# The last 64 output columns first, and two accumulators in one tile

## The chip, the cores and the metric

The kernel runs on one core of one Trainium2 chip. The metric is the device time of one execution in microseconds (us). Its engines are PE (matmuls), DVE (vector), ACT (scalar), POOL (general purpose) and SP, which here issues the DMA transfers. Matmul results land in PSUM, which has eight banks of 512 float32 per partition.

## What is computed

`x` has 8 batches of 3584 rows of 192 columns. A 7-tap convolution per head, whose weights are a softmax over the taps, gives 28672 rows, and these go through a soft mixture of 8 experts with 4 slots each (32 slots), F = 1024:

```
out    = einsum('bshk,bskhg->bshg', softmax(weight_gen), windows of x)   # -> x: 28672 x 192
logits = x @ phi                                    # 28672 x 32
d      = softmax of logits over the rows            # dispatch
slot_input = d.T @ x                                # 32 x 192
slot_out[e] = relu(slot_input[e] @ w1[e]) @ w2[e]   # per expert, 4 x 192
c      = softmax of logits over the slots           # combine
result = c @ slot_out                               # 28672 x 192
```

## The kernel before

The rows are cut into 17 units of eight pairs of groups and a short last one. In the main loop (about 25 to 217 us) each unit passes through these steps, each with its engine:

- `conv` (L263, PE) by banded weights that DVE turns (L236) from what POOL multiplied; then transposes (L283, PE).
- `logits` (L339, PE) into the PSUM tile `ls`, one bank.
- `top` (L346, DVE), `newmax` (L365, PE) and `newmax_out` (L370, DVE): the running maximum.
- `dexp` (L378, ACT): exponentials of `ls` into `dd`; `dturn` (L398, DVE): `dd` transposed into `dt`.
- `save` (L352, DVE): `ls` transposed into `LT` in the on-chip memory (SBUF), for the combine softmax later. In program order it follows `dturn` on the DVE.
- `dispatch` (L417, PE): 16 matmuls of `dt` with the unit's rows into `acb`, a PSUM tile of its own, one bank; `rescale` (L425, DVE) adds it to `accS`.

Three further tiles of two banks each, `ring0` to `ring2`, take the convolutions and transposes in turn. That fills the eight banks.

Then comes the slot stage (217 to 231.6 us), written out by hand: slot sums (L861 to L871), `hidden` (L905) in two halves u = 0, 1 with a relu and a transpose each (`turn_hidden`, L917 on PE and L918 into `hT`), `den` and `rden` (L939 to L953), the divisor, and `outputs` (L926): per expert and quarter a matmul of `hT` with `w2`, for the first DA = 128 of the D = 192 columns, into `so4`. The copy `sos` (L964), the sum over the four quarters (L968) and the scaling by `rden` (L969) give `so`.

The output stage makes 25 parts, in the order of `out_order`. A part of kind 0 is 128 columns of one half batch, one of kind 1 the last 64 columns of two half batches; both fill 128 partitions. A part is `rows` (L994, PE, into two PSUM tiles `two` of two banks, four of them in turn), `evict` (L1000, copies by ACT and DVE into free SBUF) and `store` (L1005, issued by SP; the first three parts in two stores each). The last 64 columns (`others`, `other_sums`) are made behind the fifth and sixth part. Between them stand the last combine softmaxes: maximum L92 (DVE), difference L94 (POOL), exponential L97 (ACT), sum L100 (DVE), L102 (ACT), reciprocal L104 (DVE), product L106 (POOL), and `turn` (L475, DVE), which transposes a half batch into `cT` for `rows`.

The order on the engines in the loop and in the output stage comes from a planner: every step is declared by `op(engine, cost, reads, writes, ...)`, `times` lays them on the engines by these costs, and the steps are written in the order of their planned times. Each engine runs its instructions in that order. Waits between engines are set by the framework, from which tiles an instruction reads and writes.

Of the kernel before, what the change touches and what calls it, by code (L numbers as in the profile page):

```python
# [8 lines left out]
F32 = mybir.dt.float32  # L9
# [27 lines left out]
FILL = 2  # L37
WGAP = 0.9
TR = 3 * 32 + T
RESTAT = 4  # L40
BEHIND = 6
ROUNDS = {"TE": 8, "SP": 12}
VSUM = ()
# [13 lines left out]
def conv_soft_moe(ctx, tc, xh, wh, phi, w1a, w1b, w2a, w2b, out):  # L57
# [16 lines left out]
    big = keep.tile([128, NXS * XB], F32, name="big")  # L74
    FC = F // 128
    WE = FC * D
    W2B = E * FC * DA

    DG = NS + SE
    si = keep.tile([128, E * NS + E // 2 * DG], F32, name="si")  # L80
# [43 lines left out]
    tms = [fix.tile([128, UP, 2 * (D + 1)], F32, name=f"tm{i}") for i in range(NTM)]  # L124
    tms.append(wide.rearrange("p b j -> p (b j)")[:, 0 : TAIL * 2 * (D + 1)].rearrange("p (n c) -> p n c", c=2 * (D + 1)))
    dd = fix.tile([128, 2 * UP, 32], F32, name="dd")
    ls = ps_fix.tile([128, 2 * UP, 32], F32, name="ls")


    acb = ps_fix.tile([128, 512], F32, name="acb")  # L130
    qnegP = acb[:, 264:268]

    banks = [ps_fix.tile([128, 2, 512], F32, name=f"ring{i}") for i in range(NRING)]
# [342 lines left out]
                    LT[:, g0 : g0 + n].rearrange("p g j -> p (g j)"))  # L476

    def w2_at(e, f, b):
        o = W2B * b + (e * FC + f) * (D - DA if b else DA)
        return big[:, o : o + (D - DA if b else DA)]  # L480

    def loadw1(j):
        e, f = j // 4, slice(F // 4 * (j % 4), F // 4 * (j % 4 + 1))
        to, w, e = (w1a_sb, w1a, e) if e < E else (w1b_sb, w1b, e - E)
        SY.dma_start(to[:, e, f], w[:, e, f])

    W2S = [(0, i * 4 * DA, 4 * DA) for i in range(2 * E)]
# [363 lines left out]
    half = F // 8  # L851

    spare = [banks[(used[0] + 1 + i // 2) % NRING][:, i % 2] for i in range(4)]
    homes = {"b1": acb, "b3": spare[0], "b4": spare[1], "b2": spare[2], "b0": spare[3]}

    def bank(tag, n, name):
# [84 lines left out]
    rden = pb.tile([128, 1], F32, name="rden")  # L941
    hidden(1, E // 2, E + E // 2)
# [19 lines left out]
    soft(pc, h + 1, 6)
    soft(pc, h + 2, 3)
    V.tensor_copy(sos[:, 0:DA], so4)  # L964
    soft(pc, h + 2, 4)
    soft(pc, h + 2, 5)
    sor = bank("b2", DA, "sor")
    P.matmul(sor, sel4.rearrange("p q s -> p (q s)"), sos[:, 0:DA], start=True, stop=True)  # L968
    V.tensor_scalar_mul(so, sor, rden[:, 0:1])  # L969
    soft(pc, h + 2, 6)  # L970
    turn(1, 0)
    bctx.close()


    ps_o = ctx.enter_context(tc.tile_pool(name="ps_o", bufs=4, space=PSUM))
# [6 lines left out]
    assert RESTAT + 2 < len(spots)  # L982
    spots += [big[:, i * OW : (i + 1) * OW] for i in range(E * WE // OW)]
    parts = list(out_order())
    pos, left = {}, [0]

    def rows(kind, b, g, n, j):
        pos[j] = [ps_o.tile([128, 2, 512], F32, tag="two", name=f"two{j}_{i}") for i in range(2)]
        for half in range(1 + kind):
            g0 = NG * (b + half) + g  # L990
            of = (so, sob)[kind]
            m = of.shape[1]
            for q in range(4):
                P.matmul(pos[j][q // 2][m * half : m * half + m, q % 2, 0 : n * T],  # L994
                         of[32 * q : 32 * q + 32],
                         cT[32 * q : 32 * q + 32, g0 : g0 + n, 0:T], start=True, stop=True)
# [12 lines left out]
    extra = []

    def others(u):
        if u == 0:
            extra.append(ps_o.tile([128, 2, D - DA], F32, tag="two", name="extra"))
        outputs(extra[0][:, 0], 1, (u,), 0, E)

    def other_sums():
        P.matmul(extra[0][:, 1], sel4.rearrange("p q s -> p (q s)"), sos[:, DA:D], start=True, stop=True)

    ops.clear()
    writer.clear()  # L1020
    readers.clear()
    op(VE, 0.74, [], [("cT", 3)], turn, 1, 1)
    for x in range(EARLY + 3, len(HALVES)):
        for step, (e, c) in enumerate(((VE, 0.72), (PO, 1.13), (AC, 0.66), (VE, 0.72),
                                       (AC, 0.3), (VE, 0.25), (PO, 1.13))):
            op(e, c, [], [("soft", x), ("rm", x % 2)], soft, pc, x, step)
        op(VE, 0.74, [("soft", x)], [("cT", x)], turn, x // 2, x % 2)
    twos = [0]

    def turn_two():  # L1030
        twos[0] += 1
        return ("two", twos[0] % 4)

    for j, (kind, b, g, n) in enumerate(parts):
        two, to = [turn_two(), turn_two()], ("spot", j % len(spots))
        op(TE, (1.1 + 0.8 * kind) * (n + 6) / 24, [("cT", 2 * (b + half) + (g >= STEPS[1][0])) for half in range(1 + kind)]
           + ["sob"] * kind, two, rows, kind, b, g, n, j)
        cuts = ((0, 2, AC), (2, 4, VE)) if j < 3 else ((0, 2, AC), (3, 4, VE), (2, 3, AC))
        free = ["w2"] * (j >= RESTAT + 2)
        for lo, hi, e in cuts:  # L1040
            if e == AC:
                op(AC, 0.14 + 0.4 * (hi - lo) * n / 18, [two[lo // 2], *free], [(to, lo)], evict, j, n, lo, hi, A.copy)
            else:
                op(VE, 0.12 + 0.52 * (hi - lo) * n / 18, [two[1], *free], [(to, lo), ("ev", j)], evict, j, n, lo, hi, V.tensor_copy)
        if 4 <= j + 2 < EARLY + 3:
            op(VE, 0.74, [("ev", j)], [("cT", j + 2)], turn, (j + 2) // 2, j % 2)
# [3 lines left out]
        if j == RESTAT:  # L1050
            rest = turn_two()
            op(TE, 1.05, [], [rest], others, 0)
        elif j == RESTAT + 1:
            op(TE, 1.05, [], [rest, "w2"], others, 1)
            op(AC, 0.22, [rest], ["sos"], lambda: A.copy(sos[:, DA:D], extra[0][:, 0]))
            op(TE, 0.4, ["sos"], [rest], other_sums)
            op(VE, 0.22, [rest], ["sob"], lambda: V.tensor_scalar_mul(sob, extra[0][:, 1], rden[:, 0:1]))
# [95 lines left out]
```

## Time and profile before

| | |
|---|---|
| median of 3 runs | 295.62 us (295.34 to 295.69) |
| profiled execution, its own time | 294.6 us |
| its span, first to last instruction | 292.5 us |
| busy share of PE, DVE, ACT, POOL | 88%, 73%, 62%, 55% |
| written to HBM | 22.36 MB |
| mean granted clock of PE | 0.949 |

A granted clock of 1.00 is the full 2.4 GHz, 0.50 is 1.2 GHz. Rows of a timeline give start and length in us from the span's start; a bracket at the end is the idle time of the engine before the row, and what ended it. Where several instructions of one kind follow each other, one row holds them, with their count behind an x.

### The profile page before, as it was taken

How to read it: one execution, taken by the hardware profiler on the slowest of the kernel's cores; microseconds unless marked ns; L12 is line 12 of the kernel's file. 1: busy time of each engine (PE TensorE's matmuls, PEld its weight loads, DVE VectorE, ACT ScalarE, POOL GpSimd, SP SyncE). 2: the span in 40 equal slices, each digit the busy share in tenths (PEclk: the TensorE clock that was granted, in tenths of full speed). 3: DMA queues.
4: the chain of work that ended last, by engine and by line, in shares of the span. 5: the costliest groups of instructions: out<-in, count | busy, mean ns of one | idle time of the engine just before them, and what ended most of it. 6: DMA issues, size and time to landing. Idle time of an engine off the chain costs nothing.

```text
span 292.5 us, 16099 instructions
## 1 busy us (share of the span) xinstructions
PE 258.0 (88%) x6996; PEld 209.2 (72%) x6996; DVE 212.7 (73%) x385; ACT 180.9 (62%) x307; POOL 160.4 (55%) x253
## 2 busy tenths in 40 slices
PE   8789998999899999999999999999989798856520
PEld 4579898888799898988988898998869553311100
DVE  8776999876998887788858688773374888977310
ACT  8868657576577756656665666665322378968430
POOL 9974869468496775657374735720034415555100
PEclk9999999999999999999999999999999889975675
DMA  6986677677667766767777668666988099999994
GB/s 178 233 220 175 189 230 205 175 214 211 198 174 205 215 201 192 209 187 211 223 220 207 201 196 232 187 199 168 303 269 288 14 385 407 416 423 413 416 413 185
DMA packets 30406, 70.11 MB, mean 240 GB/s; under 512 B 5760, under 2 KB 17024, under 8 KB 30336
## 3 DMA queue, kind: packets, MB, share of 16 engines
q1 hardware_dynamic: 30336, 69.08, 74.3%
q8 instruction: 55, 0.90, 1.3%
q14 instruction: 15, 0.12, 0.1%
HBM read 46.70 MB, written 22.36 MB: 236 GB/s over the span
## 4 chain that ended last, share of the span: by engine, by line
PE 74%; issue 5%; ACT 4%; DMA 4%; POOL 4%; DVE 3%; POOLq 0%; ACTq 0%
PE ring L263 33%; PE ring L283 16%; PE ls L339 8%; PE acb L417 7%; PE two L994 6%; PE ring L905 2%; DMA taps<-wh 2%; DMA out<-w1b_sb 2%; ACT big L1000 1%; POOL big L433 1%; ACT w1a_sb L1000 1%; DMA out<-w1a_sb 1%; POOL LT L106 1%; DVE band L236 1%; ACT w1b_sb L1000 1%
## 5 line engine op out<-in xcount | busy, mean ns | idle before, releaser
L263 PE MATMUL ring<-big,band 128*26 128x96 f32 x4480 | 109.7, 248 | 3.9 <-DVE band L236 2.0
L263 PEld LDWEIGHTS ring<-big,band 128*26 128x26 f32 x4480 | 99.5, 130 | 13.3 <-issue 6.8
L271 ACT COPY tm<-ring 128x768 f32<-128x768 f32 x68 | 54.5, 801 | 57.9 <-PE ring L263 45.2
L236 DVE STREAM_TRANSPOSE band<-wide 128x832 f32<-128x832 f32 x70 | 70.6, 1025 | 4.6 <-POOL wide L227 3.3
L283 PE MATMUL ring<-ident,tm 122*128 122x122 f32 x408 | 50.4, 273 | 0.8 <-issue 0.8
L227 POOL TENSOR_TENSOR wide<-taps,sum 128x364 f32<-128x364 f32 x32 | 31.4, 982 | 25.9 <-DVE sum L218 10.2
L289 ACT COPY cm<-ring 128x624 f32<-128x624 f32 x68 | 44.1, 691 | 1.9 <-PE ring L283 1.9
L283 PEld LDWEIGHTS ring<-ident,tm 122*128 122x128 f32 x408 | 42.3, 141 | 3.7 <-issue 0.9
L196 POOL TENSOR_TENSOR taps<-taps,top 128x364 f32<-128x364 f32 x34 | 32.9, 974 | 4.4 <-DVE top L188 4.2
L994 PE MATMUL two<-cT,so 32*128 32x442 f32 (+2 forms) x136 | 23.0, 701 | 11.6 <-DVE cT L475 3.9
L212 POOL TENSOR_TENSOR si<-taps 128x208 f32<-128x208 f32 x34 | 21.8, 640 | 19.9 <-ACT taps L204 19.4
L188 DVE TENSOR_REDUCE top<-taps 128x52 f32<-128x364 f32 x34 | 27.9, 822 | 4.2 <-DMA taps<-wh 4.1
L94 POOL TENSOR_TENSOR LT<-LT,rm 128x576 f32<-128x576 f32 (+1 forms) x16 | 18.1, 1133 | 20.5 <-DVE rm L92 20.3
L339 PE MATMUL ls<-cm,phi_sb 128*32 128x208 f32 x544 | 27.2, 338 | 0.0
L417 PE MATMUL acb<-tm,dt 128*32 128x193 f32 x544 | 25.8, 328 | 0.0
L994 PEld LDWEIGHTS two<-cT,so 32*128 32x128 f32 x136 | 9.2, 224 | 23.1 <-ACT w1a_sb L1000 8.3
L106 POOL TENSOR_TENSOR LT<-LT,sm 128x576 f32<-128x576 f32 (+1 forms) x16 | 18.1, 1134 | 13.1 <-DVE sm L104 13.1
L204 ACT ACTIVATE taps<-taps 128x364 f32<-128x364 f32 (+1 forms) x36 | 18.0, 503 | 7.9 <-POOL taps L196 7.0
L218 DVE RECIPROCAL sum<-sum 128x52 f32<-128x52 f32 (+1 forms) x36 | 16.3, 454 | 8.9 <-POOL sum L214 8.6
L339 PEld LDWEIGHTS ls<-cm,phi_sb 128*32 128x32 f32 x544 | 17.5, 109 | 4.2
L1000 ACT COPY big<-two 128x884 f32<-128x884 f32 (+3 forms) x26 | 17.2, 738 | 4.4 <-issue 3.5
L346 DVE TENSOR_REDUCE mx<-ls 128x1 f32<-128x416 f32 x17 | 9.8, 577 | 13.7 <-PE ls L339 12.4
(135 smaller groups left out, 298.4 us busy)
## 6 DMA issues: line engine op xcount, KB each, us to landing
big<-xh SPq DMA_DIRECT2D x224, 120.0 KB, 3.6
taps<-wh SPq DMA_DIRECT2D x35, 182.0 KB, 3.7
out<-big SPq DMA_DIRECT2D x7, 884.0 KB, 9.1
out<-big SPq DMA_DIRECT2D x6, 936.0 KB, 9.4
w1a_sb<-w1a SPq DMA_DIRECT2D x32, 128.0 KB, 3.4
big<-w2a SPq DMA_DIRECT2D x16, 256.0 KB, 4.3
out<-w1a_sb SPq DMA_DIRECT2D x3, 936.0 KB, 10.7
w1b_sb<-w1b SPq DMA_DIRECT2D x16, 128.0 KB, 3.3
```

Source lines behind the costliest of these rows:

```text
L188: V.tensor_reduce(out=row(m), in_=run(c, 0, KT).rearrange("p k s -> p s k"), axis=AX.X, op=ALU.max)
L196: eng.tensor_tensor(out=t, in0=t, in1=rows7(tops.pop((c, 0))), op=ALU.subtract)
L227: eng.tensor_tensor(out=dst, in0=raw[c % NTAP][:, 0:KT], in1=m.unsqueeze(1).to_broadcast([128, KT, n, T]), op=ALU.mult)
L236: V.transpose(bands[c % NBAND][:, b].rearrange("p b j l -> p (b j l)"), wide[:, b].rearrange("p b j -> p (b j)"))
L263: P.matmul(cv[32 * blk : 32 * blk + T, p % 2, o : o + 4 * GW], bands[g // 8 % NBAND][:, g // 4 % CH, :, i], xbd[:, place(t), :, b * GW : ( ...
L271: copy(tms[tm_at(u)][:, pr + of.start : pr + of.stop, 1 : 2 * D + 1], cv[:, of, 0 : 2 * D])
L283: P.transpose(pt[:, j // 3, o : o + TR], tm[0:TR, pr + j // 3, 1 + o : 129 + o], ident[0:TR, 0:TR])
L289: copy(cm.rearrange("p (a i) (b j) -> p a (i b) j", i=3, j=T), pts["t", k][:, of, 0 : 3 * 128].rearrange("p a (i j) -> p a i j", j=32)[... ...
L339: P.matmul(lp[32 * blk : 32 * blk + 32, lo:hi, par, 0:T], phi_sb[:, 2 * par + i, :], cm[:, lo:hi, 1 if i else 2 * par, blk, :], start=(i = ...
L417: P.matmul(ac[32 * q : 32 * q + 32], dt[:, g, :], tm[:, g // 2, o : o + D + 1], start=(g < 4), stop=(g + 4 >= 2 * n))
L994: P.matmul(pos[j][q // 2][m * half : m * half + m, q % 2, 0 : n * T], of[32 * q : 32 * q + 32], cT[32 * q : 32 * q + 32, g0 : g0 + n, 0:T] ...
L1000: copy(to.rearrange("p (q c) -> p q c", c=n * T), pos[j][lo // 2][:, lo % 2 : lo % 2 + hi - lo, 0 : n * T])
```

## The change

`ls` and `acb` become the two banks of one tile `pair`, which stays through the output stage. `den` moves from a ring bank to a column of `acb`'s bank, and `rden` is computed earlier. `outputs` makes the last 64 columns first; the first 128 are summed up in `held`, a ring tile, in pieces: four experts of the first half between those matmuls, the rest in front of the rows and between the rows of the first four parts; the copy, sum and scaling for them follow by `op`. `out_order` begins with two half-batch pairs of kind 1 (five parts). The first five parts use three PSUM tiles in turn (two ring tiles and `pair`), the later ones also `held`. `w2b` (64 columns) is loaded ahead of `w2a`.

```diff
-    bctx = ExitStack()
-    ps_fix = bctx.enter_context(tc.tile_pool(name="ps_fix", bufs=1, space=PSUM))
+    ps_fix = ctx.enter_context(tc.tile_pool(name="ps_fix", bufs=1, space=PSUM))
...
-    ls = ps_fix.tile([128, 2 * UP, 32], F32, name="ls")
-    acb = ps_fix.tile([128, 512], F32, name="acb")
+    pair = ps_fix.tile([128, 2, 512], F32, name="pair")
+    ls = pair[:, 0].rearrange("p (g j) -> p g j", j=32)
+    acb = pair[:, 1]
...
-    W2S = [(0, i * 4 * DA, 4 * DA) for i in range(2 * E)]
-    W2S += [(1, i * FC * (D - DA), FC * (D - DA)) for i in range(E)]
+    W2S = [(1, i * FC * (D - DA), FC * (D - DA)) for i in range(E)]
+    W2S += [(0, i * 4 * DA, 4 * DA) for i in range(2 * E)]
...
+    held = banks[used[0] % NRING]
+    twos = [banks[(used[0] + 1) % NRING], pair, banks[(used[0] + 2) % NRING], held]
...
-    den = bank("b3", 4 * NS + 1, "den")[:, 4 * NS :]
+    den = acb[:, 256:257]
...
-    outputs(so4, 0, (0,), 0, E // 2)
+    outputs(so4, 1, (0,), 0, E)
     turn_hidden(1)
-    outputs(so4, 0, (0,), E // 2, E)
-    outputs(so4, 0, (1,), 0, E)
+    outputs(held[:, 0, 0:DA], 0, (0,), 0, 2)
+    outputs(so4, 1, (1,), 0, E)
+    outputs(held[:, 0, 0:DA], 0, (0,), 2, 4)
...
-        pos[j] = [ps_o.tile([128, 2, 512], F32, tag="two", name=f"two{j}_{i}") for i in range(2)]
+        pos[j] = [twos[i] for i in homes_of[j]]
...
+    turns = {0: [4], 1: [6], 2: [5, 7]}
+    later_sums = {1: [(0, 5, E)], 2: [(1, 0, E // 2)], 3: [(1, E // 2, E)]}
...
+        for u, lo, hi in later_sums.get(j, ()):
+            op(TE, 0.22 * (hi - lo), [], [two(3), "w2"], outputs, held[:, 0, 0:DA], 0, (u,), lo, hi)
+        if j == 3:
+            op(AC, 0.3, [two(3)], ["sos"], lambda: A.copy(sos[:, 0:DA], held[:, 0, 0:DA]))
+        if j == 4:
+            op(TE, 0.4, ["sos"], [two(3)], other_sums)
+            op(VE, 0.3, [two(3)], ["so"], lambda: V.tensor_scalar_mul(so, held[:, 1, 0:DA], rden[:, 0:1]))
...
-    for kind, e in ((0, 0), (0, 1), (0, 2), (0, 3), (1, 0), (0, 4), (1, 2), (0, 5), (0, 6),
-                    (1, 4), (0, 7), (1, 6)):
+    for kind, e in ((1, 0), (1, 2), (0, 0), (0, 1), (0, 2), (0, 3), (0, 4), (0, 5),
+                    (1, 4), (0, 6), (0, 7), (1, 6)):
```

On PE, at the dispatch of unit 2 in the main loop, with the engines that each row waits for (DVE_49 and the like are their semaphores); before, then after:

```order
95 L263 MATMUL ring_91<-big,band_84 26x96 x31
96 L417 MATMUL acb<-tm_86,dt_1134 32x193 [waits DVE_49]
97 L417 MATMUL acb<-tm_86,dt_1134 32x193 x15
```

```order
94 L261 MATMUL ring_90<-big,band_84 26x96 x31
95 L415 MATMUL pair<-tm_86,dt_1133 32x193 [waits DVE_49,Activation_49]
96 L415 MATMUL pair<-tm_86,dt_1133 32x193 x15
```

The order is the same, and the dispatch has one wait more, since its tile is now also that of the logits, which ACT and DVE read. The row names the engine that it waits for, not the instruction: with the DVE it was `dturn` before, and is `save`, the DVE's next instruction, now.

On PE, from the second half of the hidden layer to the first rows (`so4` lies in the last ring tile of each list; `held` is ring_90); before, then after:

```order
217 L926 MATMUL ring_93<-big,hT 32x128 x16
218 L917 MATMUL ring_92<-ident,hs_4733 128x128
219 L926 MATMUL ring_93<-big,hT 32x128 x48
220 L968 MATMUL ring_93<-sos,sel_106 128x128
221 L994 MATMUL two_0_4941<-cT,so 128x234 x2
```

```order
217 L928 MATMUL ring_92<-big,hT 32x64 x32
218 L919 MATMUL ring_91<-ident,hs_4732 128x128
219 L928 MATMUL ring_90<-big,hT 32x128 x8
220 L928 MATMUL ring_92<-big,hT 32x64 x32
221 L928 MATMUL ring_90<-big,hT 32x128 x8
222 L970 MATMUL ring_92<-sos,sel_105 128x64
223 L928 MATMUL ring_90<-big,hT 32x128 x4
224 L993 MATMUL ring_91<-cT,sob 64x234 x2
```

Behind the second transpose stood 48 matmuls of 128 columns; now 32 of 64 columns, with 8 and 8 and 4 of 128 columns around them.

On DVE, from the scaling that the first rows wait for to the fourth part's eviction; before, then after:

```order
303 L969 TENSOR_SCALAR so<-ring_93,rden 128x128
304 L475 STREAM_TRANSPOSE cT<-LT 128x576
305 L1000 COPY w1a_sb<-two_1_4942 128x468
306 L475 STREAM_TRANSPOSE cT<-LT 128x544
307 L1000 COPY w1a_sb<-two_1_4948 128x468
308 L1000 COPY w1a_sb<-two_1_4959 128x884
309 L475 STREAM_TRANSPOSE cT<-LT 128x576
310 L1000 COPY w1a_sb<-two_1_4970 128x468
311 L1000 COPY w1b_sb<-two_1_4979 128x442
```

```order
302 L972 TENSOR_SCALAR sob<-ring_92,rden 128x64
303 L473 STREAM_TRANSPOSE cT<-LT 128x544
304 L999 COPY w1a_sb<-pair 128x468
305 L473 STREAM_TRANSPOSE cT<-LT 128x576
306 L999 COPY w1a_sb<-ring_91 128x468
307 L473 STREAM_TRANSPOSE cT<-LT 128x576
308 L100 TENSOR_REDUCE sm_5014<-LT 128x17
309 L999 COPY w1a_sb<-ring_92 128x884
310 L104 RECIPROCAL sm_5014<-sm_5014 128x17
311 L473 STREAM_TRANSPOSE cT<-LT 128x544
312 L999 COPY w1a_sb<-pair 128x468
313 L473 STREAM_TRANSPOSE cT<-LT 128x544
```

Ahead of the third eviction (884 columns) stand a turn and a sum L100 more than before, ahead of the fourth a reciprocal more; the two evictions of the fifth part's tiles follow further back.

## Rows read from the trace of the kernel before

**Rows 1.** Waits of PE, 20 to 209 us: total, times, longest.
```profile
PE acb L365 <- DVE mq L348: 1.4, 1, 1.4
```

**Rows 2.** Timeline of PE, units 3, 9, 15: start, length, engine, line, tiles.
```profile
64.83 0.67 PE L417 MATMUL acb<-tm,dt 128*32 128x193 f32 x12
...
135.31 1.19 PE L417 MATMUL acb<-tm,dt 128*32 128x193 f32 x24
...
203.37 0.67 PE L417 MATMUL acb<-tm,dt 128*32 128x193 f32 x12
```

**Rows 3.** Timeline of DVE, the same three units.
```profile
64.19 0.67 DVE L352 STREAM_TRANSPOSE LT<-ls 128x512 f32<-128x512 f32 x1
...
133.62 1.04 DVE L236 STREAM_TRANSPOSE band<-wide 128x832 f32<-128x832 f32 x1
134.58 0.68 DVE L398 STREAM_TRANSPOSE dt<-dd 128x512 f32<-128x512 f32 x1
135.17 0.68 DVE L352 STREAM_TRANSPOSE LT<-ls 128x512 f32<-128x512 f32 x1
...
202.91 0.68 DVE L352 STREAM_TRANSPOSE LT<-ls 128x512 f32<-128x512 f32 x1
```

**Rows 4.** Timeline of all engines, slot stage to the first rows, 217 to 232.
```profile
217.60 0.71 DVE L352 STREAM_TRANSPOSE LT<-ls 128x512 f32<-128x512 f32 x1
...
217.74 0.41 PE L861 MATMUL acb<-selE,accS 128*128 128x32 f32 x2
...
222.65 0.28 PE L939 MATMUL ring<-accS,selE 128*128 128x1 f32 x2
...
222.92 0.29 DVE L918 COPY hT<-acb 128x128 f32<-128x128 f32 x1 [0.17 <-PE acb L917]
...
226.51 0.27 ACT L918 COPY hT<-ring 128x128 f32<-128x128 f32 x1 [0.84 <-PE ring L917]
226.81 0.16 DVE L952 TENSOR_SCALAR rden<-ring 128x1 f32<-128x1 f32 x1 [3.20 <-ACT hT L918]
...
230.33 0.28 DVE L964 COPY sos<-ring 128x128 f32<-128x128 f32 x1
...
231.60 2.49 PE L994 MATMUL two<-cT,so 32*128 32x234 f32 x18 [0.44 <-DVE so L969]
```

**Rows 5.** Windows: busy us of each engine, PEclk, DMA share, GB/s.
```profile
232.10:235.50 3.40, 3.40 (x26) 2.04 (x21) 2.48 (x5) 1.73 (x3) 0.14 (x1) 0.50 0.51 184
235.50:237.00 1.50, 1.50 (x16) 0.60 (x8) 1.50 (x3) 1.20 (x2) 0.00 (x0) 0.99 0.87 337
...
245.00:287.00 42.00, 24.81 (x200) 7.70 (x196) 24.71 (x44) 28.26 (x49) 14.55 (x13) 0.75 1.01 415
```

**Rows 6.** Timeline of SP: issues of the first and the fifth store.
```profile
232.95 0.35 SPq L1005 DMA_DIRECT2D out<-w1a_sb  x1
...
235.79 0.33 SPq L1005 DMA_DIRECT2D out<-w1a_sb  x1
```

**Rows 7.** Groups by form, 231 to 293: busy us, mean ns, idle before.
```profile
L1000 ACT COPY big<-two 128x936 f32<-128x936 f32 x6 | 5.7, 944 | 0.5 <-ACT big L1000 0.5
...
L475 DVE STREAM_TRANSPOSE cT<-LT 128x576 f32<-128x576 f32 x7 | 5.4, 766 | 0.0
...
L1000 ACT COPY big<-two 128x468 f32<-128x468 f32 x6 | 3.4, 566 | 0.0
L1000 DVE COPY w1a_sb<-two 128x468 f32<-128x468 f32 x5 | 3.0, 609 | 0.2 <-PE two L994 0.2
...
L100 DVE TENSOR_REDUCE sm<-LT 128x17 f32<-128x544 f32 x4 | 2.8, 709 | 0.9 <-ACT LT L97 0.9
L97 ACT ACTIVATE LT<-LT 128x576 f32<-128x576 f32 x4 | 2.8, 708 | 0.1
...
L926 PE MATMUL extra<-big,hT 128*32 128x64 f32 x128 | 2.2, 220 | 0.0
...
L1000 DVE COPY w1a_sb<-two 128x884 f32<-128x884 f32 x1 | 1.1, 1079 | 0.8 <-PE two L994 0.8
```

More of the change, by code (lines that the diff above doesn't have):

```diff
@@ L39 @@
 TR = 3 * 32 + T
-RESTAT = 4
+RESTAT = 5
 BEHIND = 6
@@ L76, in conv_soft_moe @@
     WE = FC * D
-    W2B = E * FC * DA
+    W2A = E * FC * (D - DA)
     DG = NS + SE
@@ L478, in w2_at @@
     def w2_at(e, f, b):
-        o = W2B * b + (e * FC + f) * (D - DA if b else DA)
-        return big[:, o : o + (D - DA if b else DA)]
+        n = D - DA if b else DA
+        o = W2A * (1 - b) + (e * FC + f) * n
+        return big[:, o : o + n]
     def loadw1(j):
@@ L930, in conv_soft_moe @@
     hidden(0, 0, E // 2)
-    so4 = bank("b0", DA, "so4")
+    DB = D - DA
+    so4 = bank("b0", DB, "so4")
     hidden(0, E // 2, E + E // 2)
@@ L941, in conv_soft_moe @@
     rden = pb.tile([128, 1], F32, name="rden")
+    V.tensor_scalar_add(rden, den, EPS)
+    V.reciprocal(rden, rden)
     hidden(1, E // 2, E + E // 2)
     relu(1)
-    outputs(so4, 0, (0,), 0, E // 2)
+    outputs(so4, 1, (0,), 0, E)
     turn_hidden(1)
-    outputs(so4, 0, (0,), E // 2, E)
-    outputs(so4, 0, (1,), 0, E)
+    outputs(held[:, 0, 0:DA], 0, (0,), 0, 2)
+    outputs(so4, 1, (1,), 0, E)
+    outputs(held[:, 0, 0:DA], 0, (0,), 2, 4)
     sos = pb.tile([128, D], F32, name="sos")
     so = pb.tile([128, DA], F32, name="so")
-    sob = pb.tile([128, D - DA], F32, name="sob")
+    sob = pb.tile([128, DB], F32, name="sob")
     soft(pc, h, 5)
-    V.tensor_scalar_add(rden, den, EPS)
-    V.reciprocal(rden, rden)
     soft(pc, h, 6)
@@ L957, in conv_soft_moe @@
     soft(pc, h + 1, 3)
-    turn(0, 1)
+    turn(1, 0)
     soft(pc, h + 1, 4)
@@ L962, in conv_soft_moe @@
     soft(pc, h + 1, 6)
[L963 to L975, printed above, removed]
+    turn(0, 1)
+    V.tensor_copy(sos[:, DA:D], so4)
+    sor = bank("b2", DB, "sor")
+    P.matmul(sor, sel4.rearrange("p q s -> p (q s)"), sos[:, DA:D], start=True, stop=True)
+    outputs(held[:, 0, 0:DA], 0, (0,), 4, 5)
+    V.tensor_scalar_mul(sob, sor, rden[:, 0:1])
     OW = 4 * 18 * T
@@ L981, in conv_soft_moe @@
     spots += [big[:, NXS * XB - OW :]]
-    assert RESTAT + 2 < len(spots)
+    assert RESTAT + 1 < len(spots)
     spots += [big[:, i * OW : (i + 1) * OW] for i in range(E * WE // OW)]
@@ L1007, in store @@
         left[0] += w
[L1009 to L1014, printed above, removed]
     def other_sums():
-        P.matmul(extra[0][:, 1], sel4.rearrange("p q s -> p (q s)"), sos[:, DA:D], start=True, stop=True)
+        P.matmul(held[:, 1, 0:DA], sel4.rearrange("p q s -> p (q s)"), sos[:, 0:DA], start=True, stop=True)
+    homes_of = [[i % 3 for i in (2 * j, 2 * j + 1)] for j in range(RESTAT)]
+    order = [3] + [i % 3 for i in range(2 * RESTAT, 2 * RESTAT + 3)]
+    homes_of += [[order[i % 4] for i in (2 * j, 2 * j + 1)] for j in range(len(parts) - RESTAT)]
     ops.clear()
@@ L1022, in conv_soft_moe @@
     op(VE, 0.74, [], [("cT", 3)], turn, 1, 1)
-    for x in range(EARLY + 3, len(HALVES)):
+    for x in range(EARLY + 2, len(HALVES)):
         for step, (e, c) in enumerate(((VE, 0.72), (PO, 1.13), (AC, 0.66), (VE, 0.72),
                                        (AC, 0.3), (VE, 0.25), (PO, 1.13))):
[L1026 to L1032, printed above, removed]
+            if x > EARLY + 2 or step > 2:
+                op(e, c, [], [("soft", x), ("rm", x % 2)], soft, pc, x, step)
+        if x > EARLY + 2:
+            op(VE, 0.74, [("soft", x)], [("cT", x)], turn, x // 2, x % 2)
@@ L1034, in conv_soft_moe, with two @@
+    def two(i):
+        return ("two", i)
+    turns = {0: [4], 1: [6], 2: [5, 7]}
+    later_sums = {1: [(0, 5, E)], 2: [(1, 0, E // 2)], 3: [(1, E // 2, E)]}
     for j, (kind, b, g, n) in enumerate(parts):
-        two, to = [turn_two(), turn_two()], ("spot", j % len(spots))
-        op(TE, (1.1 + 0.8 * kind) * (n + 6) / 24, [("cT", 2 * (b + half) + (g >= STEPS[1][0])) for half in range(1 + kind)]
-           + ["sob"] * kind, two, rows, kind, b, g, n, j)
+        t, to = [two(i) for i in homes_of[j]], ("spot", j % len(spots))
+        op(TE, 1.15 * (n + 3) / 21, [("cT", 2 * (b + half) + (g >= STEPS[1][0])) for half in range(1 + kind)]
+           + ["so"] * (1 - kind), t, rows, kind, b, g, n, j)
@@ L1038, in conv_soft_moe @@
         cuts = ((0, 2, AC), (2, 4, VE)) if j < 3 else ((0, 2, AC), (3, 4, VE), (2, 3, AC))
-        free = ["w2"] * (j >= RESTAT + 2)
+        free = ["w2"] * (j > RESTAT)
         for lo, hi, e in cuts:
             if e == AC:
-                op(AC, 0.14 + 0.4 * (hi - lo) * n / 18, [two[lo // 2], *free], [(to, lo)], evict, j, n, lo, hi, A.copy)
+                op(AC, 0.14 + 0.4 * (hi - lo) * n / 18, [t[lo // 2], *free], [(to, lo)], evict, j, n, lo, hi, A.copy)
             else:
-                op(VE, 0.12 + 0.52 * (hi - lo) * n / 18, [two[1], *free], [(to, lo), ("ev", j)], evict, j, n, lo, hi, V.tensor_copy)
@@ L1045, in conv_soft_moe @@
-        if 4 <= j + 2 < EARLY + 3:
-            op(VE, 0.74, [("ev", j)], [("cT", j + 2)], turn, (j + 2) // 2, j % 2)
+                op(VE, 0.12 + 0.52 * (hi - lo) * n / 18, [t[1], *free], [(to, lo), ("ev", j)], evict, j, n, lo, hi, V.tensor_copy)
+        for x in turns.get(j, ()):
+            op(VE, 0.74, [("ev", j), ("soft", x)], [("cT", x)], turn, x // 2, x % 2)
         for lo, hi in ((0, 2), (2, 4)) if j < 3 else ((0, 4),):
@@ L1049, in conv_soft_moe @@
                store, j, n, lo, hi, late=2.0)
[L1050 to L1057, printed above, removed]
+        for u, lo, hi in later_sums.get(j, ()):
[5 more added lines that the diff above has]
+            op(VE, 0.3, [two(3)], ["so"], lambda: V.tensor_scalar_mul(so, held[:, 1, 0:DA], rden[:, 0:1]))
     at = times({TE: 0.0, VE: 0.65, AC: 0.0, PO: 0.0, SP: 0.0}, SP)
@@ L1065, in out_order @@
     cut = ((0, 18), (18, 17))
-    for kind, e in ((0, 0), (0, 1), (0, 2), (0, 3), (1, 0), (0, 4), (1, 2), (0, 5), (0, 6),
-                    (1, 4), (0, 7), (1, 6)):
+    for kind, e in ((1, 0), (1, 2), (0, 0), (0, 1), (0, 2), (0, 3), (0, 4), (0, 5),
+                    (1, 4), (0, 6), (0, 7), (1, 6)):
         for g, n in cut:
-            if (kind, e, g) == (0, 0, 0):
-                yield from ((0, 0, 0, 9), (0, 0, 9, 9))
+            if (kind, e, g) == (1, 0, 0):
+                yield from ((1, 0, 0, 9), (1, 0, 9, 9))
             else:
```

5 lines of the change are left out of this document (3 added, 2 removed).

## The prediction

> **What bounds the kernel now.** I read the page's slices first, then the idle times of the engines with what ended them, then single stretches instruction by instruction, and last the DMA share by stage. Three stages have three limits.
>
> From 25 to 217 us the tensor engine (PE) bounds. In the stretch 20 to 209 us it hardly waits for another engine: the one such entry is 1.4 us for the vector engine (DVE), once [rows 1]. The dispatch of a unit (L417, into `acb`) never waits. But look at how close the DVE runs behind it. In unit 3 the dispatch starts at 64.83 [rows 2] and the DVE's `save` of the same unit (L352, reading `ls`) runs from 64.19 for 0.67, to 64.86 [rows 3]. In unit 9 it is 135.31 against an end at 135.85, in unit 15 203.37 against 203.59 [rows 2, 3]. I read the same pair for the units 2 to 15: in nine (3, 4, 6, 8, 9, 10, 12, 13, 15) the save ends after the dispatch has begun, by 0.04, 0.39, 0.22, 0.24, 0.54, 0.29, 0.47, 0.38 and 0.22 us, 2.79 in all; in the others it ends up to 0.6 us before.
>
> From 217 to 231.6 us a chain of short steps between PE, DVE and ScalarE (ACT) bounds: slot sums, two hidden layers, two transposes, output matmuls, the sum over quarters, then the first rows at 231.60 [rows 4].
>
> From there the stores bound. 22.36 MB leave; from 245 to 287 us the share of DMA is 1.01 at 415 GB/s [rows 5], and the stretch from 235.5 to 237 is the last with a hole: a share of 0.87 leaves 0.13 of its 1.5 us, 0.2 us. The end therefore moves with two things: when the first store is issued (232.95 [rows 6]) and how many microseconds the queue stands empty before it is full for good.
>
> **The change part by part.** The time of the profiled execution is 294.6 us, 1.0 below the median of the runs shown; I sum against 294.6 and add the sum to 295.62.
>
> *The shared tile, main loop.* `ls` and `acb` become two banks of one tile, `pair`. The order of the loop's instructions is unchanged, but what they wait for is not: a wait is set for a tile, not for a bank. The dispatch writes `pair` and so waits for the `save` that reads `pair`, where before it waited for the earlier turn of the weights. That the program does guard so can be seen in a row of before: `rden`, which reads one column of a bank, stands idle 3.20 us until ACT has copied another part of that bank (L918) [rows 4]. Price: nine units' 2.79 us, and 0.05 from the DVE's end to PE's start for each (in unit 9 PE starts 0.05 after the turn's end, 134.58 + 0.68 = 135.26 [rows 3]), 3.24 in all. Queued behind the waiting dispatch are the next unit's convolutions on PE, which is the bound, so it is path. Against it: where the save is late because the DVE first had a transposition of `band` to do (unit 9: 133.62 for 1.04, ahead of the turn [rows 3]; unit 12 alike), a PE that has fallen behind finds the DVE further ahead, and the 0.54 and 0.47 with their two 0.05 may go. I take 3.24 - 1.1 = 2.1. The lower bound is 0 (all nine absorbed, since the other engines have idle time), the upper 3.24 and the 1.4 us for unit 1, where the save now waits for the whole dispatch and the row nearest is the one wait of PE for the DVE [rows 1].
>
> The Trainium skill, PSUM — Partial Sum Buffer, section PSUM bank collisions raise a hardware error, says that semaphores should guard PSUM by bank and quadrant (by bank in the simple form), not by address. By that rule these waits are not needed, and a guard by bank would leave this term at 0; the rows of before cannot show which guard the new tile gets, the `rden` row says the coarser one.
>
> *The shared tile, slot stage.* The slot sums (L861, 217.74) now wait for the last save (217.60 for 0.71, to 218.31): 0.62 with the hop. `den` moves into `pair` and waits for the copy of hT (222.92 for 0.29, to 223.21) where it began at 222.65 [rows 4]: 0.62 again, in front of the second hidden layer. Together 1.24, on the chain.
>
> *64 columns first.* Before, from the end of the second hT copy (226.51 for 0.27, 226.78) to the copy of the sums at 230.33 [rows 4] pass 3.55 us: three quarters of the 128-wide outputs, and then a DVE that has a softmax step first. Now one half of the 64-wide outputs stands there; the 128 records of that form took 2.2 us, at 220 ns [rows 7], so 64 take 1.10. The copy, the sum over quarters and the scaling keep their 1.27 (230.33 to 231.60). So the first rows come at 226.78 + 1.24 + 1.10 + 1.27 = 230.4; with 0.1 for a DVE that is in a turn, 230.5 against 231.60. Eviction and issue behind the first rows took 1.35 (231.60 to 232.95), at the half clock (0.50) that followed the gap in front of the rows [rows 5]; that gap is shorter and has matmuls in it now, so I take 1.1: first store at 231.6, 1.35 us earlier than 232.95.
>
> *The first five stores.* A part of either kind has the same bytes. But what the DVE does between their evictions is more: the order shows, from the first rows on, a turn, the first eviction, a turn, the second, a turn, a sum L100, the third (884 columns), a small step, a turn, p3's eviction, a turn, two L92, p4's. With 0.75 per turn, 0.63 and 1.08 per eviction, 0.7 per L100 or L92, 0.25 for the small step [rows 7] from 230.45: DVE evictions end at 231.95, 233.4, 236.0, 237.65 and 240.35. ACT's third copy of p3 and p4 reads the same tile behind the DVE's (in the trace of before it waits for it), 0.57 more: 238.2 and 240.9. p5 stands on ACT behind two L97 at 0.7, a 936 copy at 0.94 and a 468 copy at 0.57: about 243.8. The issues are thus some 231.6, 231.95, 232.3, 233.4, 234.4, 236.0, 238.2, 240.9, 243.8.
>
> At 415 GB/s a store of 234, 442, 936 or 884 KB lasts 0.56, 1.07, 2.26, 2.13 us; the flow begins 0.8 after the issue (before: 232.95 to about 233.75). Laid end to end this gives holes of 0.1, 0.45, 0.53, 1.1, 0.44 and 0.77, 3.4 us. The same recipe on before gives 0.59 for its fifth store (235.79 + 0.8 against 236.0 [rows 6]), where the row shows 0.2: it overstates a hole by 0.4. With 0.4 off each hole the sum is 1.2. I take the middle, 2.3, less before's 0.2, less the 1.35 of the earlier start: +0.75 (bounds -0.35 and +1.85). If the holes stayed at 0.2 it would be -1.35.
>
> The held matmuls between the rows cost PE 0.5 to 1 us each time, and PE has that room: a part's rows need some 0.9 us at full clock and the DVE needs 1.5 or more between parts. [...]
>
> *The rest.* Loads of `w2` change places with equal sizes; the last six pieces are now ones needed later. Sum of the other edits: 0.
>
> Sum: +2.1 + 0.75 = about +2.9: 294.6 becomes 297.5, and on the median 298.5 us.
>
> **The rivals.**
> Faster: the main loop absorbs the stalls, because the DVE gets ahead within a few units, and the queue is filled without new holes. For it: the DVE is not the bound and can run ahead, and the first store does come earlier. Against it: in the units 8, 10, 13 and 15 the turn starts right behind ACT's exponentials, which wait for PE's own logits, so that a later PE makes a later save. It decides where stalls left and holes together stay under 1.35: 295.62 - 1.35 + 0.4 = 294.7.
>
> Tail alone: the waits of the loop cost nothing, be it that the guard goes by bank or that all is absorbed, and the holes are as forecast: 295.62 + 0.75 = 296.4; without the slot stage's 1.24 as well, 295.1.
>
> All at its upper end: 3.24 + 1.4 and 1.85: 302.1.
>
> Clock: the new stop of 0.6 us in front of `den`, in the slot stage, lowers PE's granted clock as the gap in front of the first rows did (0.50 for the 3.4 us from 232.1 [rows 5]). Half of such a stretch is lost, 1.7 us: 300.2.
>
> **How the numbers follow.** Forecast 0.50, faster 0.14, tail alone 0.16, upper end 0.12, clock 0.08. The forecast's own range is 297 to 300.3. The range that should hold the time 8 times in 10 leaves out the very top and half of the faster case: 295.0 to 301.2. What a measurement of this kernel can tell from no change is about 0.2%, 0.6 us. Faster: the faster case and a little of the tail alone, 0.16. Same: part of the tail alone, 0.07. Slower: the rest, 0.77.
>
> **What would show it.** PE's dispatch with an idle time before it released by the DVE's `save` in six to nine units, 0.2 to 0.5 each; the slot stage starting some 2 us later than at 217; `den` released by the copy of hT; first rows 1.1 us closer to the end of the main loop; and a DMA share under 0.9 from the second store to the sixth part. Wrong would be: no idle time at the dispatch, a DMA share at 1.0 from the second store on, or a PE that waits for its own held matmuls between the rows.

## The result, and the profile after

| | before | after |
|---|---|---|
| median, first comparison | 295.72 us | 300.12 us |
| ratio, 95% interval | | 1.0144, 1.0104 to 1.0185 |
| second comparison, another time | 299.17 us | 300.93 us: 1.0063, 1.0028 to 1.0098 |
| third comparison | 297.94 us | 301.03 us: 1.0122, 1.0076 to 1.0168 |
| profiled execution: own time, span | 294.6, 292.5 us | 298.76, 296.8 us |

The changed kernel is slower in all three comparisons. The ratios compare the fast executions alone, the medians take all. Within one comparison the executions of the kernel before scatter by 1.4 to 2.4%, those of the changed kernel by 1.0 to 1.2%; a part of the reason stands under the last heading. The two profiled executions can be cut at the end of the last dispatch, which stands at 217.15 us before and at 221.87 after. So in these two executions the loop lost 4.72 us. From there to the end it takes 75.37 and 74.89 us: the rest won 0.48. But two further profiles of the changed kernel (e0_after and e8_after below) have 75.38 and 75.58 us there, so the 0.48 is a matter of this one execution.

The loop first. These are the longest waits of PE from 20 to 209 us in the changed kernel (total, times, longest); they answer to [rows 1]:

```profile
PE pair L415 <- DVE LT L350: 2.7, 8, 0.7
PE ring L261 <- issue: 2.2, 6, 0.7
PE pair L363 <- DVE mq L346: 0.5, 1, 0.5
```

The first row was not there before: the dispatch waits for the DVE's `save`. Now the timeline of unit 9, PE and then DVE, to be laid beside [rows 2, 3]:

```profile
136.82 0.70 PE L415 MATMUL pair<-tm,dt 128*32 128x193 f32 x12 [0.60 <-DVE LT L350]
```

```profile
135.40 0.67 DVE L396 STREAM_TRANSPOSE dt<-dd 128x512 f32<-128x512 f32 x1
136.00 0.67 DVE L350 STREAM_TRANSPOSE LT<-pair 128x512 f32<-128x512 f32 x1
```

The save ends at 136.67, and PE starts 0.15 later. Before, PE had started 0.05 behind the turn, while the save ran. The 0.15 is no accident: I read the pair in all 14 units from 2 to 15, and each dispatch starts 0.15 behind the end of its save, those too that show no idle time, like unit 7:

```profile
112.98 0.54 PE L415 MATMUL pair<-tm,dt 128*32 128x193 f32 x8
```

```profile
112.16 0.67 DVE L350 STREAM_TRANSPOSE LT<-pair 128x512 f32<-128x512 f32 x1
```

112.16 + 0.67 = 112.83, and 0.15 more is 112.98. Such units look free of waits, but they have lost something: undisturbed, the dispatch's first matmul starts some 0.18 us before the last matmul of the convolutions has ended (units 2 to 8 and 10 to 15 of before). Here are the convolutions ahead of the dispatch of unit 3 in the kernel before, which starts at 64.83 [rows 2], and of unit 7 in the changed kernel:

```profile
64.26 0.75 PE L263 MATMUL ring<-big,band 128*26 128x96 f32 x27
```

```profile
112.09 0.93 PE L261 MATMUL ring<-big,band 128*26 128x96 f32 x36
```

They end at 65.01 and 113.02, so the overlap is 0.18 before and 0.04 after. (A profile models the ends of matmuls; the comparison counts, not the single value.)

Unit 2 waits as well, 0.68 us, although its save ended 0.58 ahead of the dispatch before. In the units 0 and 1 the save now has to wait for the whole dispatch, and the DVE stands idle for it, in unit 1 for 1.41 us. This is what the forecast's upper bound had for unit 1; that it makes the save of unit 2 late is likely, but not tested.

Not all of the 4.72 us lies in the stretch in which dispatches wait. 1.10 is lost ahead of the dispatch of unit 1 (at 40.73 before, 41.83 after), 2.97 from there to the dispatch of unit 15 (203.37 and 207.44), and 0.65 behind that, where a stop of 0.99 for PE's own instructions stands at 218.01. In the middle stretch the idle time and the lost overlap in front of the 14 dispatches come to 5.0 us more than before; PE's other stops over 0.15 us are 2.2 us fewer (1.4 against 3.6).

Then the slot stage, in the timeline of all engines, against [rows 4]:

```profile
222.33 0.71 DVE L350 STREAM_TRANSPOSE LT<-pair 128x512 f32<-128x512 f32 x1
...
223.09 0.41 PE L863 MATMUL pair<-selE,accS 128*128 128x32 f32 x2 [0.58 <-DVE LT L350]
...
228.27 0.29 DVE L920 COPY hT<-pair 128x128 f32<-128x128 f32 x1 [0.17 <-PE pair L919]
...
228.61 0.38 PE L942 MATMUL pair<-accS,selE 128*128 128x1 f32 x2 [0.45 <-DVE hT L920]
...
232.29 0.27 ACT L920 COPY hT<-ring 128x128 f32<-128x128 f32 x1 [0.84 <-PE ring L919]
...
233.03 1.97 PE L928 MATMUL ring<-big,hT 128*32 128x128 f32 x94 [0.44 <-issue]
...
235.75 0.41 PE L993 MATMUL ring<-cT,sob 32*64 32x234 f32 x2
```

Both forecast waits are there, released by the save and by the copy of hT. Counted from the end of the last dispatch, the slot sums start at 1.22 instead of 0.59, `den` at 6.74 instead of 5.50, and the first rows at 13.87 instead of 14.45: 0.58 earlier, not 1.1. A stop of 0.44 that nobody had on the list stands in between ("issue": PE waited for nothing that the profile shows).

The stores, in windows, against [rows 5] (length, busy time of PE, of its weight loads, of DVE, ACT and POOL, then the granted clock, the share of DMA and GB/s):

```profile
237.00:242.00 5.00, 4.93 (x122) 2.75 (x126) 4.95 (x9) 2.14 (x5) 0.94 (x1) 1.00 0.70 257
242.00:249.00 7.00, 5.75 (x64) 2.64 (x56) 5.45 (x10) 6.09 (x12) 2.38 (x3) 1.00 0.93 374
...
292.00:294.00 2.00, 0.00 (x0) 0.00 (x0) 0.00 (x0) 0.00 (x0) 0.00 (x0) 0.50 0.68 277
294.00:296.77 2.77, 0.00 (x0) 0.00 (x0) 0.00 (x0) 0.00 (x0) 0.00 (x0) 0.50 0.05 20
```

and the same stretches of the kernel before, from its first store (232.95) and at its end:

```profile
233.00:238.00 5.00, 5.00 (x92) 3.21 (x88) 4.24 (x8) 3.08 (x5) 0.00 (x0) 0.75 0.81 307
238.00:245.00 7.00, 5.55 (x108) 3.01 (x98) 6.55 (x13) 5.62 (x11) 3.42 (x3) 1.00 1.02 410
...
288.00:290.00 2.00, 0.00 (x0) 0.00 (x0) 0.00 (x0) 0.00 (x0) 0.00 (x0) 0.50 0.24 96
290.00:292.50 2.50, 0.00 (x0) 0.00 (x0) 0.00 (x0) 0.00 (x0) 0.00 (x0) 0.50 0.03 11
```

The first twelve microseconds have more holes than before: 0.30 * 5 + 0.07 * 7 = 2.0 us not used, against 0.19 * 5 - 0.02 * 7 = 0.8. But at the end the queue stays full for longer: 0.24 and 0.03 before, 0.68 and 0.05 after. PE ran the first rows at the full clock (1.00 in every window from 217 to 249), where before it had the half (0.50 from 232.1 to 235.5 [rows 5]).

### The profile page after: what moved, and what is told of

It reads as the page before. It is cut to its first block, busy times and chain, and to the rows that moved or that the text cites. A ratio compares the mean times of both kernels' runs of the same rounds, so it can differ in the third digit from the quotient of the medians.

```text
span 296.8 us, 16133 instructions
## 1 busy us (share of the span) xinstructions
PE 260.2 (88%) x7004; PEld 211.8 (71%) x7004; DVE 212.9 (72%) x385; ACT 180.7 (61%) x307; POOL 160.2 (54%) x253
## 5 line engine op out<-in xcount | busy, mean ns | idle before, releaser
L261 PE MATMUL ring<-big,band 128*26 128x96 f32 x4480 | 111.1, 248 | 5.4 <-DVE band L234 2.5
L261 PEld LDWEIGHTS ring<-big,band 128*26 128x26 f32 x4480 | 101.1, 129 | 14.3 <-issue 7.0
L234 DVE STREAM_TRANSPOSE band<-wide 128x832 f32<-128x832 f32 x70 | 70.6, 1025 | 3.5 <-POOL wide L225 2.2
L993 PE MATMUL ring<-cT,so 32*128 32x442 f32 (+1 forms) x96 | 22.3, 729 | 13.9 <-DVE cT L473 7.5
L415 PE MATMUL pair<-tm,dt 128*32 128x193 f32 x544 | 26.5, 329 | 2.9 <-DVE LT L350 2.7
L337 PE MATMUL pair<-cm,phi_sb 128*32 128x208 f32 x544 | 27.2, 338 | 0.0
L993 PEld LDWEIGHTS ring<-cT,so 32*128 32x128 f32 x96 | 7.3, 224 | 26.3 <-ACT sm L102 8.8
L415 PEld LDWEIGHTS pair<-tm,dt 128*32 128x32 f32 x544 | 19.2, 109 | 6.0 <-ACT al L402 3.5
L337 PEld LDWEIGHTS pair<-cm,phi_sb 128*32 128x32 f32 x544 | 17.5, 109 | 4.2
L344 DVE TENSOR_REDUCE mx<-pair 128x1 f32<-128x416 f32 x17 | 9.8, 575 | 13.4 <-PE pair L337 13.4
```

What stands on the lines that cost most here:

```text
L234: V.transpose(bands[c % NBAND][:, b].rearrange("p b j l -> p (b j l)"), wide[:, b].rearrange("p b j -> p (b j)"))
L261: P.matmul(cv[32 * blk : 32 * blk + T, p % 2, o : o + 4 * GW], bands[g // 8 % NBAND][:, g // 4 % CH, :, i], xbd[:, place(t), :, b * GW : ( ...
L337: P.matmul(lp[32 * blk : 32 * blk + 32, lo:hi, par, 0:T], phi_sb[:, 2 * par + i, :], cm[:, lo:hi, 1 if i else 2 * par, blk, :], start=(i = ...
L415: P.matmul(ac[32 * q : 32 * q + 32], dt[:, g, :], tm[:, g // 2, o : o + D + 1], start=(g < 4), stop=(g + 4 >= 2 * n))
```

## The experiments

**The changed kernel again** (e0_after, e8_after), no edit.

> The changed kernel once more, on the same chip as the next three. Theory (the shared tile costs time, in the main loop above all): the ratio to the kernel before is again 1.010 to 1.018, about +3 to +5 us. Rival (the first execution was a disturbed one): within 0.5% of before.

> The changed kernel beside the next two on one chip. Theory: 0.6 to 1.4% slower than before, with 13 or 14 dispatches that start 0.15 us behind the end of the save. Rival: the loss seen so far belongs to single executions, and the ratio includes 1.

Measured: 1.0063 (1.0028 to 1.0098) and 1.0122 (1.0076 to 1.0168). Slower both times, in the first by less than the 1.010 expected. Both profiles show the wait for the save again, 1.5 and 1.6 us in six times each, and starts 0.15 behind the save's end in 13 and 11 of the 14 units; in the others the dispatch was late by itself. In unit 9 of both, a stop of PE for its own instructions (1.23 and 0.97 us) ends just ahead of the dispatch, which then does not wait.

**Two tiles again** (e1_split, e6_split_again): the only change to the changed kernel is that `ls` and `acb` are tiles of their own, allocated behind the ring tiles and given back behind the slot stage.

```diff
-    pair = ps_fix.tile([128, 2, 512], F32, name="pair")
-    ls = pair[:, 0].rearrange("p (g j) -> p g j", j=32)
-    acb = pair[:, 1]
...
+    bctx = ExitStack()
+    ps_two = bctx.enter_context(tc.tile_pool(name="ps_two", bufs=1, space=PSUM))
+    ls = ps_two.tile([128, 2 * UP, 32], F32, name="ls")
+    acb = ps_two.tile([128, 512], F32, name="acb")
...
+    bctx.close()
+    ps_o = ctx.enter_context(tc.tile_pool(name="ps_o", bufs=1, space=PSUM))
+    pair = ps_o.tile([128, 2, 512], F32, name="pair")
```

> The changed kernel with `ls` and `acb` as two tiles again; they are given back behind the slot stage and `pair` is a new tile for the rows. Theory: PE's 2.7 us of waiting for the save go, with about 0.15 for each restart, and 0.6 us in front of the slot sums: 4.5 to 5 us less than the changed kernel, 294.5 to 295.5 on the scale of before's 295.7. The wait of `den` for the copy of hT stays, since both lie in `acb`. Rival (the loop's loss is a late start or the moved weights' loads, and the waits are only where that shows): within 1.5 us of the changed kernel.

> The two split tiles once more, since the first run's times scattered by some 2% and its profile was a disturbed one. Theory: 0.7 to 1.4% less than the changed kernel's ratio, so 0.995 to 1.000 of before. From the last dispatch's end to the end of the kernel 75.0 us, against 75.4 in before.

Measured: 0.9993 (0.9957 to 1.0029) and 0.9989 (0.9955 to 1.0023). The loss is gone, and nothing is won over before. From the last dispatch to the end 74.72 us in e6. In the same comparison as e1 the changed kernel had 1.0063: the shared tile cost 0.7% there, 2.1 us, half of what the first comparison shows and less than half of the 4.5 to 5 us expected.

**The shared tile alone** (e2_before_pair): the kernel before, with `ls` and `acb` as the two banks of one tile.

> The kernel before with `ls` and `acb` as banks of one tile, nothing else changed. Theory: 4 to 5 us slower than before (14 dispatches wait for the save, the slot sums too), 299.7 to 300.7. Rival (the loss belongs to the reordered outputs and stores): within 1 us of before.

Measured: 1.0071 (1.0033 to 1.0109), +1.5 us by the medians, +2.1 by the ratio. The sign is the theory's; the size is 1.5 to 2.1 us where I expected 4 to 5. Its waits, 20 to 209 us:

```profile
PE ring L262 <- issue: 3.4, 7, 0.7
PE pair L416 <- DVE LT L351: 1.4, 4, 0.7
```

The wait for the save appears in the old kernel by this edit alone. It is smaller than in the profile above (1.4 against 2.7), while PE's stops for its own issue are longer.

**The same shared tile, another order** (e4_save_late, e9_save_late): in the changed kernel the planner is told that the save reads `accS`, which puts it behind the unit's rescale on the DVE.

```diff
-        op(VE, 0.06 * UNITS[u][1] + 0.2, [], ["ls", ("LT", u)], save, u, due=12.0)
+        op(VE, 0.06 * UNITS[u][1] + 0.2, ["accS"], ["ls", ("LT", u)], save, u, due=12.0)
```

> The changed kernel, shared tile and all, with the save of a unit put behind its rescale on the DVE, so that no dispatch waits for a save. Theory (that wait and PE's restart behind it are the price of the shared tile): no idle time of PE before the dispatch released by the save, and a time like that of the split tiles, 0.7 to 1.2% less than the changed kernel. Rival (the price lies in the other waits of a shared tile, logits behind the rescale, save behind the dispatch): as slow as the changed kernel.

> The shared tile with the save behind the rescale, on the same chip as the changed kernel and the split one. Theory (the dispatch's wait for the save is the price): the ratio lies 0.5 to 1.2% under the changed kernel's and within 0.4% of the split tiles'. Rival (a shared tile costs through its other waits): within 0.3% of the changed kernel.

Measured: 0.9965 (0.9917 to 1.0013), and, beside the changed kernel's 1.0122, 1.0023 (0.9986 to 1.0060). The DVE in unit 9 of e9:

```profile
134.37 0.67 DVE L396 STREAM_TRANSPOSE dt<-dd 128x512 f32<-128x512 f32 x1
...
137.17 0.42 DVE L423 SCALAR_TENSOR_TENSOR accS<-accS,al,pair 128x193 f32<-128x193 f32 x1 [0.85 <-PE pair L415]
137.50 0.71 DVE L350 STREAM_TRANSPOSE LT<-pair 128x512 f32<-128x512 f32 x1
```

and PE:

```profile
135.52 1.33 PE L415 MATMUL pair<-tm,dt 128*32 128x193 f32 x28
```

The dispatch begins without a wait, the save comes 2 us behind it, and in 13 of the 14 units PE has its old overlap of 0.18 again. So it is not the tile as such: it is this one instruction standing between the turn and the dispatch. With the save gone from there, the transposition of `band` (L234) comes earlier on the DVE; but between 20 and 209 us PE waits for `band` in neither kernel. What the other waits of the shared tile cost is too little for these comparisons: 1.0023 here, 0.9986 with split tiles (e10 below), intervals that overlap.

**`den` in the other bank** (e3_split_den, e10_split_den): as e1, and `den` is written to the tile of the logits.

```diff
-    den = acb[:, 256:257]
+    den = ls.rearrange("p g j -> p (g j)")[:, 0:1]
```

> As e1_split, and `den` in the bank of `ls`, which nobody reads then. Theory: the second hidden layer starts 0.5 to 0.6 us earlier behind the first transpose, so the first rows and the end come 0.5 us earlier than in e1_split. Rival (the chain is covered by the second half of the weights' loads): the same time as e1_split.

> Split tiles and `den` in the bank of `ls`, the variant with the lowest ratio so far (0.9973). Theory (the reordered outputs are worth 0.2 to 0.6 us behind the last dispatch, and nothing in the loop): 0.997 to 1.000 of before, not to be told from it. Rival: 0.995 or less, a gain over the kernel before.

Measured: 0.9973 (0.9934 to 1.0011) and 0.9986 (0.9945 to 1.0027): no gain that can be told. `den` starts at 5.50 instead of 6.11 behind the last dispatch, as forecast, but the first rows come at 13.90 and 13.48, and in e6, where `den` still waits, at 12.88. In between stands a stop of PE for its own instructions. Here is PE in e10 and in e6, at the same matmul, the tenth record of the held ones:

```profile
230.25 1.75 PE L927 MATMUL ring<-big,hT 128*32 128x128 f32 x87 [1.50 <-issue]
```

```profile
229.95 1.75 PE L927 MATMUL ring<-big,hT 128*32 128x128 f32 x87 [0.19 <-issue]
```

The stop is 1.50 us in the one and 0.19 in the other. It does not follow from how early PE comes: in the changed kernel, e0_after and e8_after PE reaches this matmul at 10.7 us behind the last dispatch each time and stops for 0.44, 0.50 and 1.12, and the first rows come at 13.87, 13.93 and 14.58. Between executions of one kernel they differ by 0.4 to 0.7 us, as much as the 0.6 that the edit was to show. So whether an earlier `den` is worth anything stays open.

**The held matmuls later** (e5_held_later): as e3, with the 20 held matmuls in front of the first rows moved behind the second part.

```diff
-    outputs(held[:, 0, 0:DA], 0, (0,), 0, 2)
...
-    later_sums = {1: [(0, 5, E)], ...
+    later_sums = {1: [(0, 0, E)], ...
```

> Split tiles, `den` in the bank of `ls`, and the 20 held matmuls that stood in front of the first rows moved behind the second part. Theory (in the profiles PE stops in this stage for its own instructions, not for data): with 20 matmuls fewer ahead of them the first rows come 0.8 to 1.0 us earlier, 12.9 to 13.1 us behind the last dispatch's end instead of 13.9. Rival (the second half of the outputs waits for something else, the loads of w2 or the DVE): rows at 13.9 as before.

Measured: 1.0022 (0.9984 to 1.0060); first rows at 13.48, not at 12.9 to 13.1. That fell: the stops for issue are there all the same, 0.7 and 0.5 us, and the third part's store is 1.1 us later (4.47 behind the first instead of 3.38 in e3), with all 32 matmuls of the first half now in front of its rows.

**Softmax behind the evictions** (e7_soft_behind): as e3, with the last softmaxes declared behind the fifth part and reading its eviction.

```diff
...
+        if j == 4:
+            for x in range(EARLY + 3, len(HALVES)):
+                late_soft(x, 0, [("ev", 4)])
```

> Split tiles, `den` in the bank of `ls`, and the maxima (L92) of the last softmaxes kept behind the fifth part's evictions on the DVE. Theory (the DVE's work between the evictions makes the holes in the stores): the store of the fifth part comes 6.6 to 7.2 us behind the first instead of 8.31, that of the sixth at 8.5 to 9.5 instead of 10.82, the share of DMA in these 5 us rises, and the end comes 0.3 to 0.8 us earlier than 74.95 us behind the last dispatch. Rival (the stores are late through PE's held matmuls): the same store times.

Measured: 1.0003 (0.9963 to 1.0043). The fifth part's store comes at 8.23 (8.31 before the edit), the sixth's at 10.38 (10.82), but the fourth's at 6.66 (5.91). That fell for the most part. The DVE's second, fourth and fifth eviction now wait for others, as the rows of the last two show:

```profile
243.35 0.65 DVE L1002 COPY w1a_sb<-pair 128x468 f32<-128x468 f32 x1 [0.17 <-ACT w1a_sb L1002]
244.30 0.62 DVE L1002 COPY w1b_sb<-ring 128x442 f32<-128x442 f32 x1 [0.30 <-PE ring L996]
```

In front of the fifth part's rows PE has 32 held matmuls (1.08 us). In the changed kernel PE has no room left there: from 238 to 244 us PE and DVE are both busy nearly throughout, one microsecond like the other (PE stands first, the DVE third).

```profile
240.00:241.00 1.00, 1.00 (x33) 0.48 (x24) 1.00 (x3) 0.61 (x2) 0.00 (x0) 1.00 0.86 322
242.00:243.00 1.00, 1.00 (x29) 0.53 (x19) 1.00 (x3) 1.00 (x3) 0.16 (x1) 1.00 1.03 410
```

That taking work from the DVE alone leaves PE as the limit fits this; no run takes work from both.

## Why the prediction was right

The forecast was slower by 2.9 us, through waits of the dispatch for the save, and the experiments bear out sign and mechanism: tile apart or save elsewhere, the loss is gone; the tile alone brings it into the kernel before. The single terms came out less well, and that the total came near is in part luck: the loop's term was too small in the profile, and of the tail's two terms both were too large, with opposite signs.

*The loop, +2.1 forecast, +4.72 in the profile.* Two pieces were too small. The price of a wait was taken as the lateness of the save and 0.05; PE starts 0.15 behind the save. With 0.15 the lateness of [rows 2, 3] and its like gives 4.4 us, since three units more are touched that had seemed just in time (5, 7 and 14). And the 1.1 taken off for the units in which the DVE was late by its own queue did not show in this profile: in unit 9 PE waited 0.60. That 4.4 lies near 4.72 is chance, though: from unit 1 to unit 15, where the dispatches wait, the loop lost 2.97, since PE's other stops were fewer, and the rest was lost where no dispatch waits for a save. In the other two comparisons the loss was 0.6 and 1.2%, 1.8 to 3.7 us. Their profiles have more stops of PE's own ahead of waits (unit 9), and that part of the waits fell into them is a reading of those two profiles.

*Bank or tile.* The rival in which the tile's waits cost nothing is out. The row of `rden` [rows 4] could not decide between bank and tile: in the kernel before, `den` and the part that ACT copied lie in one bank, so a guard by bank would make that wait too. What decides is the dispatch: it writes the second bank of `pair` and waits for the save, which reads the first. By the rule on guarding by bank in the Trainium skill, PSUM — Partial Sum Buffer, section PSUM bank collisions raise a hardware error, these waits were not needed. The kernel before agrees: in unit 9 its dispatch writes one bank from 135.31 on while the save reads another until 135.85 [rows 2, 3]. The kernel with two tiles, 0.9989 to 0.9993 of before, shows what a guard by bank would be worth here.

*The slot stage, +1.24.* To the hundredth: 0.63 for the slot sums, 0.61 more for `den`, the same in e0 and e8. But what `den`'s share is worth at the first rows is not shown: e3 and e10 took both waits away, and the rows came no earlier than in e6, where `den` still waits. The stop for PE's own instructions was next in line, which the forecast had not named.

*First store 1.35 earlier.* It was 0.63 earlier (15.17 behind the last dispatch instead of 15.80). The stop of 0.44 in front of the second half of the outputs is most of the difference; the way from the first rows to the store took 1.29 us instead of 1.1. With the longer stops of e0 and e8 (0.50 and 1.12) the first store came at 15.22 and 15.87: in e8 nothing of the gain was left. The 1.10 us for the outputs was also too small, since held matmuls stand around them: from the second copy of hT to the copy of the sums it took 1.64 us where no such stop came (e7). Against that, the second copy of hT ended 1.05 us later than before rather than 1.24, and from the copy of the sums to the rows it took 1.13 instead of 1.27 and 0.1.

*The holes, +2.1 over before.* The store times behind the first were close: 5.91, 8.31 and 10.82 us for the fourth to sixth part, against the 6.6, 9.3 and 12.2 forecast. The holes grew by 1.2, near the lower of my two bounds (whose holes, with 0.4 off those above 0.4, add up to 1.3, not 1.2). The forecast's reason was the DVE alone; it gave PE room, and PE had none (6.00 of the 6 us from 238 to 244). And a hole did not cost what it lasted: from the first store to the end it took 59.57 us before and 59.72 after, 60.16 in e0 and 59.71 in e8, so the new holes cost 0.1 to 0.6 us. About 0.8 us came back at the end, where the queue stays full for longer. The whole tail, forecast +0.75, was -0.48, 0.0 and +0.2 in the three profiles. That some of the DMA engines lag and catch up in the holes fits this, but was not tested.

*Clock.* The rival did not happen: the granted clock is 1.00 in the slot stage and in the first rows, with both waits in it.

*What stays open.* The size of the whole: of 1.0144, 1.0063 and 1.0122 the first two have intervals that do not meet (1.0104 and 1.0098). A comparison tells some 0.4%, not the 0.2% that the forecast took from three runs. PE's own stops change from execution to execution, and how much of the waits they swallow on average is not shown.

## What to carry to other kernels

Before two buffers are put into one tile, list for each engine which instruction now stands between a producer and its consumer: an order that was harmless becomes a wait, and here moving one instruction behind the consumer took it away. A slack of zero in the trace is not free: count from the end of the other engine's instruction to the first start that was seen behind such a wait, and count the overlap that is lost. And cut two profiles at one common event, but take more than one profile of each: here the cut at the last dispatch split a loss of 4.2 us into +4.7 and -0.5, and two more profiles of the same kernel showed that the -0.5 was not the kernel's.

## What the runs showed of the hardware

PE stops for its own instructions, as far as the profiles show it. Its idle times put down to issue end 1.2 to 1.7 us behind the end of a transfer on the instruction queue: all 126 that last over 0.15 us, between 20 and 240 us of the thirteen profiles, in the changed kernel at 145.25 and 218.01 among others. Such transfers come about every 4 us, so by chance some one in eight would end in a stretch of 0.5 us.

```profile
145.25 0.49 PE L261 MATMUL ring<-big,band 128*26 128x96 f32 x13 [0.50 <-issue]
```

```profile
218.01 0.38 PE L337 MATMUL ring<-cm,phi_sb 128*32 128x26 f32 x23 [0.99 <-issue]
```

The DMA view of 215.4 to 216.8 us has the one packet that precedes the second (queue, packets, MB, share of 16 engines):

```profile
q1 hardware_dynamic: 197, 0.35, 83.3%
q8 instruction: 1, 0.02, 4.2%
```

It began at 215.6 and took 0.95 us, like the 55 of the whole execution (0.9 to 1.7 us, 16 KB, about every 4 us); PE went on 1.45 us behind its end. The stop in front of the outputs is of this kind: packet 230.8 to 231.8, PE on at 233.03. The transfers of this queue take their share of the same 16 DMA engines as the loads (the two rows above). The loop's time differs from execution to execution: the last dispatch ended at 217.15 in the one profile of before, at 218.37, 219.27, 219.56, 220.44 and 222.97 in five executions with the same loop (e3, e10, e6, e5, e7). The stops between 20 and 209 us add up to 3.2, 2.7, 1.8, 5.2, 4.1 and 4.5 us in these six, so they are a part of the difference and not all of it; what makes a transfer late was not tested.
